# A Strassen level in layer 1 of four token groups, PSUM banks seeded by copies, and an engine order from a search

## The chip, the cores and the metric

The kernel runs on one core of one Trainium2 chip. The metric is the device time of one execution in microseconds (us), and less is better. Every kernel below was timed beside the kernel before on the same chip and in the same session. Where a ratio is given, it is the mean time of one kernel's fast runs over the mean time of the other's fast runs of the same rounds, so it is not quite the ratio of the medians that stand beside it. A run counts as slow when it is over 1.5% above the fastest of its kernel; slow runs are left out of ratios.

The five engines are TensorE (PE, with PEld its weight loads), VectorE (DVE), ScalarE (ACT), POOL and SyncE (SP). In the traces of this case each took its work in the order in which the program emitted it: the changed kernel and e12, which differ in the place of two small copies on POOL, have the same sequence of all 2807 matmuls and all 451 DVE instructions, although their times differ. So an instruction that waits holds up those that stand behind it on its engine: in e14 the last ACT result before a DVE gate was there at 36.74 us, but the gate began at 39.21, behind a sum that had waited 2.52 us for its load.

## The reference, cut to what matters

```python
q_p, k_p = phi(q), phi(k)              # relu, then times cos and sin of the position
kv  = einsum('bhsf,bhsd->bhfd', k_p, v)
num = einsum('bhsf,bhfd->bhsd', q_p, kv)
den = einsum('bhsf,bhf->bhs', q_p, k_p.sum(2)) + 1e-6
x   = (num / den), heads joined        # 4608 tokens x 512
h   = x @ w_in                         # layer 1: 512 -> 2048
g   = h * cos(h)
out = g @ w_out                        # layer 2: 2048 -> 512
```

There are 8 batches of 8 heads, 576 positions and 64 features. The kernel cuts the 4608 tokens into nine groups of 512: 0 to 6, "r" (what is left of the batches) and 7. The matmuls run in 16 bits, the result is 32-bit.

## The kernel before: the parts that matter here

The program first builds a list of operations (`op`), each with the engines that may take it and a cost on each, then puts them in an order, then emits them. Before, a greedy scheduler makes the order:

```python
def run(self, cold=0.0):                        # Plan.run, cut
    while ready:
        cand = []
        for o in ready:
            t = max([o.at] + [d.end + d.lat for d in o.deps])
            ...                                 # buffers: wait for a free one
            for e, us in o.alts.items():
                cand.append((max(t, clock.get(e, 0.0)), e, us, o, t))
        t0, e0 = min((c[0], c[1]) for c in cand)
        ...                                     # earliest start, then priority
```

Layer 1 is plain in all groups: 64 matmuls of 512 columns per group. Layer 2 is a Strassen product with seven products instead of eight in all groups but the first. It needs sums of blocks of g, and all of them are DVE's:

```python
def sums(g, c, n):
    ...
    nc.vector.tensor_tensor(out=out, in0=in0, in1=in1, op=op)   # 128 x 1024, f16, both inputs in SBUF
st[(c, n)] = op({"V": 0.69}, (1, i, c, n), lambda e, c=c, n=n: sums(g, c, n), ...)
```

The seven products end in three PSUM banks. The shared product is evicted once by ACT and then added to other banks by DVE:

```python
e1 = op({"A": 0.6},  EV, lambda e: cp(e, part(g, "s1"), ps[(g, "X")]), deps=[p1], acq=[s1])
e6 = op({"V": 0.69}, EV, lambda e: add(part(g, "u2"), g, "Y", "s1"), deps=[p6, e1], ...)
...                                             # e7, e5, e4, e3: adds of DVE too
```

## Time and profile before

The time is 303.36 us (median of 3, 303.26 to 305.72).

| what | value | seen in |
|---|---|---|
| TensorE busy | 280.1 us of a span of 298.7 (94%) | the page |
| DVE, ACT, POOL busy | 233.7, 175.6, 102.0 us | the page |
| last matmul ends | 293.9 us | the trace |
| TensorE idle between matmuls after 14 us | 15.8 us, none of it after 200 us | sum over the trace |

The first lines of the page: busy time, share and number of instructions of each engine, then the busy share in tenths in 40 slices, and the clock granted to TensorE.

```profile
span 298.7 us, 6583 instructions
PE 280.1 (94%) x2565; PEld 201.3 (67%) x2565; DVE 233.7 (78%) x450; ACT 175.6 (59%) x303; POOL 102.0 (34%) x107
...
PE   8879999899969987999979999999999999999993
...
PEclk9979999999999999999999999999999999999998
```

TensorE is close to full, and its clock is whole from the fourth slice to the last but one. A change that takes matmul work away should shorten this kernel, as long as the other engines keep up.

The groups of instructions by line and form show what two kinds of DVE work cost: line, engine, operation, output and inputs, count, then busy time and mean ns.

```profile
L309 DVE TENSOR_TENSOR s<-g 128x1024 f16<-128x1024 f16 x14 | 10.4, 744 | 0.1
...
L309 DVE TENSOR_TENSOR g<-g,s 128x1024 f16<-128x1024 f16 x14 | 9.5, 704 | 0.3 <-PE PX L337 0.2
...
L181 DVE TENSOR_SCALAR kp<-km,CS 128x512 f16<-128x512 f32 x28 | 15.5, 590 | 0.3 <-DMA km<-in_k_dram 0.2
```

A sum of 1024 elements costs 0.68 to 0.74 us. TensorE's longest waits are small (what it waited for, us in total, times, longest):

```profile
PE N L228 <- DVE x L241: 2.8, 2, 2.1
PE M L279 <- ACT xT L159: 2.6, 1, 2.6
PE PY L337 <- DVE s L309: 2.2, 2, 1.6
```

### The profile page before, as it was taken

How to read it: one execution, taken by the hardware profiler on the slowest of the kernel's cores; microseconds unless marked ns; L12 is line 12 of the kernel's file. 1: busy time of each engine (PE TensorE's matmuls, PEld its weight loads, DVE VectorE, ACT ScalarE, POOL GpSimd, SP SyncE). 2: the span in 40 equal slices, each digit the busy share in tenths (PEclk: the TensorE clock that was granted, in tenths of full speed). 3: DMA queues.
4: the chain of work that ended last, by engine and by line, in shares of the span. 5: the costliest groups of instructions: out<-in, count | busy, mean ns of one | idle time of the engine just before them, and what ended most of it. 6: DMA issues, size and time to landing. Idle time of an engine off the chain costs nothing.

```text
span 298.7 us, 6583 instructions
## 1 busy us (share of the span) xinstructions
PE 280.1 (94%) x2565; PEld 201.3 (67%) x2565; DVE 233.7 (78%) x450; ACT 175.6 (59%) x303; POOL 102.0 (34%) x107
## 2 busy tenths in 40 slices
PE   8879999899969987999979999999999999999993
PEld 8768856688855555566646666776666666566782
DVE  1878888899995798887869798987786786768661
ACT  2846748599379797679489497634433443443210
POOL 1370004396191686287077194011002001100500
PEclk9979999999999999999999999999999999999998
DMA  7799995897899999999999999715202100200213
GB/s 218 264 163 203 204 362 183 279 308 120 273 274 235 356 232 169 283 278 203 322 256 202 238 369 195 141 47 151 35 0 94 48 1 32 111 2 0 91 52 140
DMA packets 77086, 53.29 MB, mean 178 GB/s; under 512 B 46080, under 2 KB 74752, under 8 KB 77056
## 3 DMA queue, kind: packets, MB, share of 16 engines
q1 hardware_dynamic: 69760, 39.73, 55.2%
q0 software_dynamic: 6848, 12.59, 16.6%
q10 hardware_dynamic: 448, 0.57, 0.5%
q8 instruction: 20, 0.33, 0.5%
q14 instruction: 10, 0.08, 0.1%
HBM read 36.74 MB, written 9.44 MB: 155 GB/s over the span
## 4 chain that ended last, share of the span: by engine, by line
PE 55%; DMA 16%; DVE 10%; POOL 5%; SPq 5%; ACT 4%; issue 3%; ACTq 0%; DVEq 0%
PE M L279 26%; DMA vm<-in_v_dram 13%; PE PY L337 8%; PE PZ L337 6%; PE PX L337 5%; PE M L376 5%; POOL qp L181 4%; DMA qm<-in_q_dram 3%; PE KV L219 2%; DVE g L292 2%; SPq L171 2%; DVE x L241 2%; PE TP L263 2%; DVE s L309 2%; SPq L269 1%
## 5 line engine op out<-in xcount | busy, mean ns | idle before, releaser
L279 PE MATMUL M<-xT,w_in_sb 128*128 128x512 f16 (+1 forms) x640 | 120.2, 336 | 2.9 <-ACT xT L159 2.6
L286 ACT ACTIVATE ch<-M 128x512 f32<-128x512 f32 x144 | 84.9, 595 | 60.8 <-PE M L279 58.7
L292 DVE TENSOR_TENSOR g<-M,ch 128x512 f16<-128x512 f32 x128 | 85.8, 687 | 27.0 <-ACT ch L286 26.1
L279 PEld LDWEIGHTS <-w_in_sb 128*128 128x128 f16 x704 | 67.3, 98 | 46.6 <-issue 3.1
L181 POOL TENSOR_SCALAR qp<-qm,CS 128x512 f16<-128x512 f32 x29 | 60.0, 2074 | 31.0 <-DMA qm<-in_q_dram 27.0
L337 PEld LDWEIGHTS <-g 128*128 128x128 f16 x560 | 54.1, 98 | 11.5
L369 POOL DMA_DIRECT2D out_dram<-ost x14 | 7.8, 558 | 98.6 <-DVE ost L351 42.5
L179 ACT ACTIVATE kp<-km,CS 128x512 f16<-128x512 f32 x52 | 35.1, 715 | 0.2
L179 ACT ACTIVATE qp<-qm,CS 128x512 f16<-128x512 f32 x40 | 26.9, 713 | 11.9 <-DMA qm<-in_q_dram 11.9
L337 PE MATMUL PX<-w_out_sb,g 128*128 128x256 f16 x224 | 27.6, 273 | 0.0
L241 DVE TENSOR_TENSOR x<-N,rec 128x512 f16<-128x512 f32 (+1 forms) x44 | 26.1, 594 | 1.7 <-DVE rec L237 0.2
L337 PE MATMUL PY<-WT,g 128*128 128x256 f16 x224 | 27.2, 273 | 0.0
L337 PEld LDWEIGHTS <-s 128*128 128x128 f16 x224 | 21.4, 98 | 7.1 <-DVE s L309 2.8
L161 POOL CAST V<-vm 128x512 f16<-128x512 f32 (+1 forms) x22 | 13.9, 664 | 15.9 <-DMA vm<-in_v_dram 15.9
L228 PE MATMUL N<-kvz,qT 128*128 128x65 f16 x256 | 14.7, 196 | 2.3 <-DVE x L241 2.1
L228 PEld LDWEIGHTS <-qT 128*128 128x128 f16 x256 | 12.6, 100 | 6.1 <-issue 3.5
L337 PE MATMUL PY<-WT,s 128*128 128x256 f16 x112 | 14.1, 273 | 2.2 <-DVE s L309 2.2
L181 DVE TENSOR_SCALAR kp<-km,CS 128x512 f16<-128x512 f32 x28 | 15.5, 590 | 0.3 <-DMA km<-in_k_dram 0.2
L292 DVE TENSOR_TENSOR gr<-M,ch 128x512 f16<-128x512 f32 x16 | 10.9, 689 | 5.7 <-ACT ch L286 5.5
L219 PE MATMUL KV<-V,kp 128*128 128x65 f16 x320 | 12.9, 196 | 2.5 <-DVE kp L181 0.7
L279 PE MATMUL M<-xR,w_in_sb 128*128 128x512 f16 x64 | 15.1, 379 | 0.0
L219 PEld LDWEIGHTS <-kp 128*128 128x128 f16 x320 | 11.7, 99 | 4.7 <-issue 2.4
(70 smaller groups left out, 287.7 us busy)
## 6 DMA issues: line engine op xcount, KB each, us to landing
out_dram<-ost POOLq DMA_DIRECT2D x28, 256.0 KB, 4.1
qm<-in_q_dram SPq DMA_DIRECT2D x8, 640.0 KB, 5.3
km<-in_k_dram SPq DMA_DIRECT2D x8, 640.0 KB, 7.0
qm<-in_q_dram SPq DMA_DIRECT2D x8, 512.0 KB, 5.8
km<-in_k_dram SPq DMA_DIRECT2D x8, 512.0 KB, 8.8
vm<-in_v_dram SPq DMA_DIRECT2D x6, 640.0 KB, 8.1
vm<-in_v_dram SPq DMA_DIRECT2D x6, 512.0 KB, 8.9
w_in_sb<-in_moe_w_in_dram POOLq DMA_DIRECT2D x4, 512.0 KB, 9.0
```

The costliest lines, as they stand in the source:

```text
L161: (nc.vector if eng == "V" else nc.gpsimd).tensor_copy(out=out, in_=in_)
L179: nc.scalar.activation(out=dst, in_=src, func=AF.Relu, scale=sc)
L181: (nc.vector if eng == "V" else nc.gpsimd).tensor_scalar(out=dst, in0=src, scalar1=0.0, scalar2=sc, op0=ALU.max, op1=ALU.mult)
L219: nc.tensor.matmul(tile_[:, n, hh, :], lhsT=kps[b][:, t, h].rearrange("p g d -> p (g d)"), rhs=V1[:, t, h, :], start=(t == 0), stop=(t == NT))
L228: nc.tensor.matmul(tile_[:, n, hh, :], lhsT=qT(p, t)[:, h, :], rhs=kvzs[p][:, h, :], start=(i == 0), stop=(i == len(parts) - 1))
L241: nc.vector.tensor_tensor(out=dst, in0=tile_[:, :, :, 0:D], in1=rec.unsqueeze(3).broadcast_to((P, nb, HB, D)), op=ALU.mult)
L279: nc.tensor.matmul(ps[key][:, n, :], lhsT=w_in_sb[:, c, j * P:(j + 1) * P], rhs=x[:, c, s0:s1], start=(c == 0 and n == 0), stop=(c == NCT ...
L286: nc.scalar.activation(out=ps[("ch", key)], in_=ps[key].rearrange("p j s -> p (j s)"), func=AF.Sin, bias=math.pi / 2.0, scale=1.0)
L292: nc.vector.tensor_tensor(out=dst, in0=m, in1=ps[("ch", key)].rearrange("p (j s) -> p j s", s=m.shape[2]), op=ALU.mult)
L337: nc.tensor.matmul(ps[(g, bank)][:, i, :], lhsT=lhs[:, j, i * P:(i + 1) * P], rhs=rhs[:, j], start=(first and i == 0 and j == 0), stop=(j ...
L369: e0.dma_start(out=five[:, t0:t0 + 2, :], in_=blocks(ost, n))
L376: nc.tensor.matmul(ps[("M2", t)], lhsT=gts[0][:, j, t * P:(t + 1) * P], rhs=w_out_sb[:, j, :], start=(j == 0), stop=(j == NJT - 1))
```

## The change

The intent has four parts. A Strassen level is put into layer 1 of the last four groups (seven products of half size for eight). The first group's layer 2 becomes Strassen too. Where a shared product was added afterwards by DVE, it is now copied into a PSUM bank by ACT or DVE, and the next matmuls add to it. And the order is no longer computed: it is a fixed text, `ORDER`, from a long annealed search. The core of the diff:

```diff
-    def run(self, cold=0.0):
-        ...                                    # the greedy scheduler
+    def run(self):
+        return [(self.ops[int(x.rstrip("VAG"))], x.lstrip("0123456789"))
+                for x in ORDER.split()]
+ORDER = """
+115 818 25 230 180 184 24 229 342 22 883 21 40V 42V 41A 44V 43A 60 46A 61V 62 63V 48A 35V 32A
+...                                            # 1481 places; V, A, G: DVE, ACT, POOL
+"""
...
+    def tt(eng, out, in0, in1, op):
+        (nc.vector if eng == "V" else nc.gpsimd).tensor_tensor(out=out, in0=in0, in1=in1, op=op)
...
-        nc.vector.tensor_tensor(out=out, in0=in0, in1=in1, op=op)      # sums
+        tt(eng, out, in0, in1, op)
...
+    STR = {5, 6, "r", 7}                       # groups with Strassen in layer 1
...
+    WSUM = {"V": 1.24, "G": 4.7}
+    XSUM = {"V": 0.42, "G": 1.3}
+    SUM0 = {"V": 0.72, "G": 2.45}              # costs of a sum on DVE and on POOL
+    CGATE = {"V": 0.7, "G": 1.3}
...
+            def y_seed(e, qd=qd):              # seeds a bank by a copy
+                bank_tile(g, qd, "Y")
+                cp(e, ps[(g, qd, "Y")], ps[(g, qd, "X")])
...
+            def z_add(e, qd=qd):
+                tt(e, ps[(g, qd, "Z")], ps[(g, qd, "Y")], ps[(g, qd, "p5")], ALU.add)
...
-    layer2_plain(lambda t, n: (1, 1, t, n))
+    layer2(0, lambda i: (1, 1, i))
```

In the order, 57 operations with two inputs, sums and gates, stand on POOL. In what follows, "order" means this text, with the choice of engine that it also makes.

## The prediction

> **What bounds the kernel now.** The page gives TensorE 94% of a 298.7 us span, VectorE (DVE) 78%, ScalarE (ACT) 59%, POOL 34%. In TensorE's timeline, steady runs take 0.216 us per matmul of 512 columns and 0.1086 per 256. By that count layer 1 is 576 x 0.216 = 124.3 us, layer 2 of the first group 64 x 0.216 = 13.8, Strassen layer 2 of eight groups 8 x 112 x 0.1086 = 97.3, attention and transposes about 27: 263 us. The stream begins at 15.8 us (loads) and ends at 294.0, so 15 of 278 us are lost. TensorE's waits name about 12 of them, all before 190 us: xT at 87-90 (2.6), sums at 110-114 (2.9), the numerator at 152 (2.1). From 190 to 281 us the windows show TensorE 100%, DVE 76%, ACT 40%. After the last matmul: 0.69 us eviction, about 4.0 us store.
>
> **What the change does.**
> 1. Layer 1 of four groups: 64 x 512 columns become 112 x 256: 13.8 -> 12.2 us, four times: -6.6 us.
> 2. Layer 2 of the first group by Strassen: -1.7 us.
> 3. Two covering matmuls: +0.4 us. [...] I expect a right result.
> 4. Per quad four more PSUM passes: 64 x 0.6 to 0.69, about +42 us on ACT and DVE. Layer 2 keeps seven evictions per group, five now plain copies that ACT can take. Counting the new order by the trace's durations: DVE 234 -> 256 us, ACT 176 -> 207.
> 5. About 42 sums (1024 elements) and 11 gates go to POOL; the trace has no such operation. [...] some DVE sums (0.70 us now) will stretch.
> 6. The searched order replaces the greedy one, with finer q buffers; I expect it to remove half of the 12 us of waits. The last eviction is split by rows: -0.4 us.
>
> **How much is critical.** TensorE is the limit nearly throughout, so 1 to 3 count fully (-7.9). The new passes lie where 24% of DVE and 60% of ACT are free, but each quad is a chain of matmul, copy, matmul, add, matmul; with DVE at 90% I expect new waits of 1 to 3 us after 190 us.
>
> **Sum.** Span: 15.8 start + 255 matmuls + 8 lost + 4.3 end = 283. The timed median stood 4.7 us above the profiled span (303.36 against 298.7); so 288 us, 5% less. Range 283.5 to 295. Chances: faster 0.94, within 2% 0.05, slower 0.01.
>
> **What would show it.** 1-2: 112 matmuls per group at 0.109 us. 4: DVE 245-265 us, ACT 200-215. 5: [...] some DVE sums above 0.75 us. 6: TensorE's waits between 16 and 190 us about 6 us; the stream starting near 16 us and ending near 278.
>
> **What would make it wrong.** POOL sums far slower than estimated, or locking DVE, so that layer 2 waits for sums (292 and more); the fixed order meeting late DMA (loads land 5 to 12 us after issue) with no freedom to do other work; or a search that removed nearly all waits (284).

The sum: 15.8 + 255 + 8 + 4.3 = 283 us of span, and 288 us of time. Neither the time of POOL's sums nor the stretching of DVE's had a term in it. That some DVE sums stretch was an expectation then; the trace after shows it (744 ns before, 1605 after).

## More of the kernel before

The profile is of a run of its own, which took 300.70 us.

No instruction of POOL has two inputs in SBUF in this kernel.

## The result, and the profile after

The result is right, and the kernel is slower: 333.21 us (median of 4, 330.40 to 335.41) against 303.31 in the same session. The ratio of the fast runs is 1.095, with a 95% interval of 1.082 to 1.108. The profile is of the slow run (335.41 us), so its span is 1 to 5 us too long for the three fast ones. The page after:

```profile
span 333.6 us, 7212 instructions
PE 289.2 (87%) x2807; PEld 229.9 (69%) x2807; DVE 269.7 (81%) x451; ACT 189.1 (57%) x349; POOL 210.0 (63%) x161
...
PE   8769953879999999999699949999999799789893
...
PEclk9979997698999999999899989999999799979998
```

TensorE is no longer full: there are holes near 50, 160 and 195 us and smaller ones near 260 and 285, and after each of them the granted clock falls too (to between 0.6 and 0.9 of full in a slice of the page, where the kernel before has 0.9 or more from the fourth slice to the last but one). The same groups as above, after the change, and the POOL sums that are new:

```profile
L340 DVE TENSOR_TENSOR g<-M,ch 128x512 f16<-128x512 f32 x102 | 67.4, 683 | 8.0 <-ACT ch L389 7.2
...
L340 POOL TENSOR_TENSOR s<-s,g 128x1024 f16<-128x1024 f16 x10 | 21.9, 2188 | 5.5 <-DVE s L340 5.1
...
L219 DVE TENSOR_SCALAR kp<-km,CS 128x512 f16<-128x512 f32 x32 | 21.4, 697 | 1.0 <-DMA km<-in_k_dram 1.0
...
L340 DVE TENSOR_TENSOR s<-g 128x1024 f16<-128x1024 f16 x9 | 14.4, 1605 | 0.2
...
L340 DVE TENSOR_TENSOR g<-g,s 128x1024 f16<-128x1024 f16 x8 | 10.0, 1248 | 0.1
...
L418 DVE TENSOR_TENSOR w_out_sb<-w_out_sb 128x1024 f16<-128x1024 f16 x2 | 5.1, 2608 | 0.0
```

The same DVE sum went from 0.74 to 1.6 us, a sum of w_out blocks takes 2.6 us, and the relu products (kp) went from 590 to 697 ns. The gates, which take one input from PSUM, kept their 683 ns (687 before). So DVE as such did not become slower. Sorting the DVE instructions of this trace by what POOL did at the same time shows the pattern (mean ns, or each value where there are few):

| DVE instruction | POOL not computing | POOL in a two-input sum | POOL in a tensor_scalar |
|---|---|---|---|
| sum s<-g, both inputs in SBUF | 691 | 1398, 3633, 5287 | 681 |
| tensor_scalar kp | 478 | 1387 (two instructions) | 707 |
| gate g<-M,ch, one input in PSUM | 686 | 682 | 681 |

The other traces say the same. Taken over all 16, DVE's sums of 1024 elements over g and s take 685 ns where POOL does nothing (307 sums, none over 694), 684 beside memsets alone (35), 795 beside a tensor_scalar alone (104; median 683, at most 1334) and 1698 beside two-input sums alone (48). So a tensor_scalar of POOL, though it reads SBUF, blocks a sum little (795 ns against 685); a POOL instruction with two inputs is what costs (1698).

The timeline shows how it happens (start, duration, engine, instruction; in brackets the idle time before it and what ended it):

```profile
40.91 2.12 POOL L340 TENSOR_TENSOR s<-s,g 128x1024 f16<-128x1024 f16 x1
...
42.14 3.63 DVE L340 TENSOR_TENSOR s<-g 128x1024 f16<-128x1024 f16 x1
...
43.12 2.11 POOL L340 TENSOR_TENSOR g<-g 128x1024 f16<-128x1024 f16 x1
...
45.83 1.05 PE L438 MATMUL PZ<-WT,s 128*128 128x256 f16 x8 [2.99 <-DVE s L340]
...
46.30 5.14 DVE L418 TENSOR_TENSOR w_out_sb<-w_out_sb 128x1024 f16<-128x1024 f16 x2
```

The DVE sum issued at 42.14 while POOL held a sum until 43.03. It did not run then either: POOL's next sum began at 43.12, and the DVE sum ended at 45.77, 0.5 us after that one. So it seems to have run only when both were over. TensorE stood for 3 us. Its longest waits after:

```profile
PE TP L311 <- DVE qp L219: 4.8, 1, 4.8
PE PX L438 <- DVE SD L199: 4.4, 1, 4.4
PE PX L438 <- DVE gr L340: 3.3, 1, 3.3
PE SD L438 <- DVE s L340: 3.3, 3, 2.1
PE PZ L438 <- DVE s L340: 3.0, 1, 3.0
```

All are waits for DVE. Two of them name neither a sum nor a gate, but a qp and a copy that seeds a bank (SD); these stood on DVE behind blocked sums, the qp behind the w_out sums of 46.30, the copy behind this one:

```profile
192.49 5.29 DVE L340 TENSOR_TENSOR s<-g 128x1024 f16<-128x1024 f16 x1
...
193.02 2.13 POOL L340 TENSOR_TENSOR s<-s,g 128x1024 f16<-128x1024 f16 x1
...
195.10 2.11 POOL L340 TENSOR_TENSOR g<-g 128x1024 f16<-128x1024 f16 x1
...
197.70 0.69 DVE L199 COPY SD<-PX 128x512 f32<-128x512 f32 x1
...
198.44 1.86 PE L438 MATMUL PX<-w_out_sb,g 128*128 128x256 f16 x8 [4.44 <-DVE SD L199]
```

This sum began 0.53 us before the first of the two POOL sums (192.49 against 193.02) and ended 0.57 us after the second. So back to back sums of POOL can hold up one DVE sum several times.

After some idle stretches TensorE ran at half clock in this trace: the record of the granted clock has 0.5 for 3.41 us from 20.32, 74.94, 163.68, 197.81, 262.67 and 293.39 us, and for 10.24 us from 54.45. Six of these seven began in or shortly after one idle stretch of TensorE: of 1.79 us (to 20.75), 4.78 (to 53.85), 2.35 (to 164.38), 4.44 (to 198.43), 2.07 (to 262.73) and 3.34 us (to 293.48). The one from 74.94 came after three short ones, 1.77 us together. No limit can be read from that: an idle stretch of 2.99 us in the same trace (to 45.83 us), and two of 2.60 and 2.12 us in the kernel before (to 89.91 and 153.91), brought none.

To add this up, I took TensorE's matmuls of each trace from 14 us on, start to start, and split that time into the columns at the steady rate of these traces (0.216 us per 512), idle stretches over 0.15 us, and what matmuls took longer because the granted clock was 0.5. "DVE blocked" is the time of DVE's instructions with all inputs in SBUF beyond their unblocked duration. All in us:

| kernel | median time | matmuls | idle | half clock | DVE blocked |
|---|---|---|---|---|---|
| before | 303.3 | 260.6 | 15.8 | 1.1 | 5.9 |
| after | 333.2 | 253.6 | 45.9 | 12.1 | 39.7 |

To name what is in the 39.7: about two thirds are sums, most of the rest relu products (kp, qp). The last matmul ends 34.8 us later in the profiled run: 7.0 us less matmul work, 30.1 more idle, 11.0 more at half clock, 0.7 of small change. The Strassen level took away what it should. The idle time gave it back four times over.

### The profile page after: what moved, and what is told of

It reads as the page before. It is cut to its first block, busy times and chain, and to the rows that moved or that the text cites. A ratio compares the mean times of both kernels' runs of the same rounds, so it can differ in the third digit from the quotient of the medians.

```text
span 333.6 us, 7212 instructions
## 1 busy us (share of the span) xinstructions
PE 289.2 (87%) x2807; PEld 229.9 (69%) x2807; DVE 269.7 (81%) x451; ACT 189.1 (57%) x349; POOL 210.0 (63%) x161
## 4 chain that ended last, share of the span: by engine, by line
PE 42%; DVE 23%; DMA 18%; issue 6%; ACT 5%; POOL 3%; SPq 1%; ACTq 0%; DVEq 0%; POOLq 0%
PE M L327 9%; PE SD L438 7%; DVE g L340 6%; DMA w_out_sb<-in_moe_w_out_dram 6%; PE M L383 5%; PE PZ L438 5%; DMA km<-in_k_dram 5%; PE PX L438 4%; PE SD L383 3%; DVE kp L219 3%; DMA out_dram<-ost 3%; DMA vm<-in_v_dram 3%; PE YZ L383 3%; ACT ch L389 2%; PE KV L255 2%
## 5 line engine op out<-in xcount | busy, mean ns | idle before, releaser
L389 ACT ACTIVATE ch<-M 128x512 f32<-128x512 f32 x108 | 63.0, 595 | 50.9 <-PE M L383 26.0
L327 PE MATMUL M<-xT,w_in_sb 128*128 128x256 f16 (+1 forms) x448 | 78.2, 324 | 3.3 <-DMA w_in_sb<-in_moe_w_in_dram 2.2
L340 DVE TENSOR_TENSOR g<-M,ch 128x512 f16<-128x512 f32 x102 | 67.4, 683 | 8.0 <-ACT ch L389 7.2
L217 ACT ACTIVATE qp<-qm,CS 128x512 f16<-128x512 f32 x44 | 29.9, 715 | 10.4 <-DMA qm<-in_q_dram 7.6
L219 POOL TENSOR_SCALAR qp<-qm,CS 128x512 f16<-128x512 f32 x14 | 28.9, 2072 | 9.4 <-DMA qm<-in_q_dram 7.0
L219 POOL TENSOR_SCALAR kp<-km,CS 128x512 f16<-128x512 f32 x12 | 25.0, 2092 | 3.4 <-DMA km<-in_k_dram 3.4
L340 POOL TENSOR_TENSOR s<-s,g 128x1024 f16<-128x1024 f16 x10 | 21.9, 2188 | 5.5 <-DVE s L340 5.1
L383 PEld LDWEIGHTS <-WS 128*128 128x128 f16 x192 | 18.9, 101 | 5.5 <-issue 1.5
L199 POOL CAST V<-vm 128x512 f16<-128x512 f32 (+1 forms) x22 | 15.3, 724 | 11.4 <-DMA vm<-in_v_dram 11.3
L340 POOL TENSOR_TENSOR g<-g 128x1024 f16<-128x1024 f16 x10 | 22.4, 2244 | 0.0
L438 PE MATMUL PZ<-WT,s 128*128 128x256 f16 x128 | 17.3, 281 | 5.3 <-DVE s L340 3.0
L219 DVE TENSOR_SCALAR qp<-qm,CS 128x512 f16<-128x512 f32 x22 | 16.9, 782 | 5.3 <-DMA qm<-in_q_dram 5.3
```

Of the source, the lines that this page charges most:

```text
L199: (nc.vector if eng == "V" else nc.gpsimd).tensor_copy(out=out, in_=in_)
L217: nc.scalar.activation(out=dst, in_=src, func=AF.Relu, scale=sc)
L219: (nc.vector if eng == "V" else nc.gpsimd).tensor_scalar(out=dst, in0=src, scalar1=0.0, scalar2=sc, op0=ALU.max, op1=ALU.mult)
L327: nc.tensor.matmul(ps[key][:, n, :], lhsT=w_in_sb[:, c, j * P:(j + 1) * P], rhs=x[:, c, s0:s1], start=(c == 0 and n == 0), stop=(c == NCT ...
L340: (nc.vector if eng == "V" else nc.gpsimd).tensor_tensor(out=out, in0=in0, in1=in1, op=op)
L383: nc.tensor.matmul(ps[(g, qd, bank)][:, i, :], lhsT=lhs[:, c, 2 * qd + i, :], rhs=rhs[:, c, :], start=(first and i == 0 and c == 0), stop= ...
```

## The experiments

Theory LOCK: POOL's sums block DVE's, and TensorE waits for DVE. Rivals: POOL itself is late with its sums; the fixed order and its chains of matmul, copy, add are worse than the greedy order even without the lock; the extra work of the level cannot be hidden at all; batch 1's loads come too late.

### e1: POOL without its sums

In the changed kernel each two-input operation of POOL becomes two tiny copies and two memsets of the output, about as long and in the same place. Its output is wrong, which doesn't matter for the time.

```diff
+        for x in (in0, in1):
+            nc.gpsimd.tensor_copy(out=out[..., 0::P], in_=x[..., 0::P])
+        for _ in range(2):
+            nc.gpsimd.memset(out, 0.01)
-        nc.gpsimd.tensor_tensor(out=out, in0=in0, in1=in1, op=op)
```

> The changed kernel with each of POOL's 57 two-input operations replaced by two tiny copies (which keep the waits for both inputs) and two memsets of the output: POOL stays busy about as long (2.1 to 2.3 us for 1024 elements), but hardly reads. Wrong result on purpose. Theory LOCK (a POOL operation that reads two SBUF tensors blocks VectorE operations with two SBUF inputs): VectorE sums back to 0.69 us, none above 1.3 us next to such a POOL operation, VectorE busy about 235 us in place of 270, TensorE gaps below 20 us in place of 36, time 292 to 305. Rival ORDER/CHAINS (the fixed order and the longer matmul-copy-matmul-add chains cost the time by themselves): time stays within 325 to 336 although the sums are short. Rival POOL-LATE (POOL is simply too slow to deliver its sums in time): time also stays above 320, since POOL is as busy as before.

Measured: 314.56 us (311.61 to 315.82), ratio 1.036 (1.029 to 1.044). POOL was no less busy (221.4 us against 210.0). DVE fell from 269.7 to 241.1 us, blocked time from 39.7 to 10.6:

```profile
L341 DVE TENSOR_TENSOR s<-g 128x1024 f16<-128x1024 f16 x9 | 6.2, 688 | 0.3
...
L346 POOL MEMSET s<- 128x1024 f16 x34 | 33.1, 973 | 2.0
```

So 18.6 us of the loss (333.2 to 314.6) go with POOL's reads, though POOL works as long as ever. But 11.6 us against the kernel before remain, where LOCK expected at most 2. TensorE's idle time is still 30.4 us, where LOCK expected less than 20. All three expectations missed: the lock is most of it, not all.

### e2: the same sums on DVE

The 57 operations get the letter V for G in the fixed order, nothing else is moved.

```diff
-155V 165 178A 171V 172 181G 166A 173 179V 199 174A 343 192V 236 200 167V 182G 175V 210 201A 238
+155V 165 178A 171V 172 181V 166A 173 179V 199 174A 343 192V 236 200 167V 182V 175V 210 201A 238
```

> The changed kernel, same order, but the 57 two-input operations of POOL run on VectorE at the same places. LOCK: VectorE's sums are 0.69 us each, but VectorE carries about 39 us more real work in place of some 34 us of blocking, so it becomes the limit itself: VectorE busy 270 to 285 us, time 320 to 335, i.e. no cure. POOL-LATE: POOL no longer delays anything, time falls below 310. ORDER/CHAINS: the same order on a fuller VectorE, time 335 or more.

Measured: right result, 318.04 us (315.35 to 320.42), ratio 1.046 (1.039 to 1.054). POOL falls to 97.9 us and DVE takes 57 instructions more, yet its busy time falls:

```profile
PE 282.3 (89%) x2807; PEld 224.7 (71%) x2807; DVE 266.5 (84%) x508; ACT 189.5 (60%) x349; POOL 97.9 (31%) x104
```

DVE does all the sums itself in 3 us less than it took for its own share beside POOL, and the kernel is 15 us faster. In this order POOL's help was worth less than nothing. All three expectations missed in the time: LOCK, by 2 us, with its 320 to 335; POOL-LATE with below 310; ORDER/CHAINS with 335 or more.

### e3 and e4: sums, or writes, added to the kernel before

The kernel before gets 64 useless POOL operations, one for every second gate from the 18th on: a sum of 1024 elements on a scratch tile (e3), or two memsets of it (e4), which read nothing.

```diff
+        count[0] += 1
+        if count[0] > 16 and count[0] % 2 == 0:
+            nc.gpsimd.tensor_tensor(out=junk, in0=junk, in1=junk, op=ALU.subtract)   # e3
+            nc.gpsimd.memset(junk, 0.25)                                             # e4, twice
```

> The kernel before, with 64 useless sums of 1024 fp16 elements on POOL, on a scratch tensor that nobody reads (one after every second gate in the order). LOCK: VectorE's sums that meet one rise from 0.68 to 1.3 us and more, while PSUM-reading gates stay at 0.69; VectorE busy up by 10 to 25 us, and the time is up by 4 to 20 us more than in the run with writes in their place. ORDER/CHAINS and POOL-LATE: the same time as the run with writes, within 2 us.

> The kernel before, with 64 pairs of memsets of 1024 fp16 elements on POOL (about 1.9 us a pair) in place of the useless sums: POOL as late, nothing read. LOCK: VectorE sums stay at 0.68 to 0.75 us, and the time is 303 to 312, what POOL's own lateness costs. POOL-LATE: as slow as the run with sums.

Measured: e3 345.08 us, ratio 1.139 (1.129 to 1.148); e4 329.45 us, ratio 1.087 (1.081 to 1.092); both results right. DVE's own sums in e3, with POOL's added ones:

```profile
L297 POOL TENSOR_TENSOR junk<-junk 128x1024 f16<-128x1024 f16 x64 | 130.0, 2032 | 2.5
...
L312 DVE TENSOR_TENSOR g<-g 128x1024 f16<-128x1024 f16 x14 | 20.9, 1495 | 0.0
```

and in e4:

```profile
L298 POOL MEMSET junk<- 128x1024 f16 x64 | 61.5, 961 | 3.7
...
L313 DVE TENSOR_TENSOR g<-g 128x1024 f16<-128x1024 f16 x14 | 9.7, 695 | 0.0
```

With POOL about equally busy (234.7 us in e3, 222.0 in e4), the reading sums block DVE by 50.9 us and the writes by 7.3 (5.9 in the kernel before). That is the lock, shown in a kernel without the change. It costs 15.6 us of time here, within the 4 to 20 that LOCK expected between the two; DVE's busy time rose by 43.0 us in e3, where 10 to 25 were expected. The other 26 us of e4 were not expected (303 to 312 us): POOL's own useful work (V, qp) comes late, and TensorE waits 8.5 us for V. A busier POOL has a price of its own where something waits for it.

### e5 and e6: the same work in an order that counts the lock

I wrote a small model of the engines with the lock and the half clock in it, and searched for an order of the changed kernel's operations. The three small marker copies on POOL that hold back batch 1's loads were put together as one operation; the work is otherwise the same, with 44 two-input operations still on POOL in e5.

```diff
+                            mark.append(op({"G": 0.55}, (0, 1), lambda e: markers(),
+                                           deps=[w_land[NG + 1]] + feats0))
-115 818 25 230 180 184 24 229 342 22 ...
+...                                            # another ORDER
```

> The changed kernel with the same arithmetic and 44 two-input operations still on POOL, but a new fixed order: searched by replaying the dependency graph with one more rule, that a VectorE operation with two SBUF inputs waits for a running two-input POOL operation, and with a half-speed TensorE after an idle gap. The three small copies that release the loads of the second batch stand together. LOCK: the loss was the collision, so an order that avoids it recovers it: VectorE excess of the sums below 12 us, TensorE gaps 15 to 28 us, time 290 to 302, below the kernel before. CHAINS (matmul-copy-matmul-add chains and a seventh product per quad cost the time by themselves): time stays at 310 or more, as in the run with writes in place of the POOL sums.

> A second order from the same search with another random start: as the first, 290 to 302 if the rule and not the luck of one order makes the difference.

Measured: e5 311.47 us (ratio 1.025, 1.019 to 1.031), e6 321.03 us (1.054, 1.047 to 1.060). Both are faster than the changed kernel by 12 to 22 us and both miss what LOCK expected; CHAINS's "310 or more" fits both. The blocked time of DVE fell to 11.0 and 23.0 us (e6's profile is of a slow run, so its figure is a hint only). I found a fault in my search: a transfer could take a place that its issuing instruction did not have.

### e7 and e8: transfers tied to their issue

> The changed kernel's work once more, every matrix product, sum, copy and transfer (only the three small marker copies on POOL that release the batch-1 loads stand together as one, as in e5), in a second order of my own. The search for e5 and e6 had let a transfer start at a place in the order that its issuing instruction did not have, so those two orders were worse on the chip than in the search (296 to 300 us when evaluated properly, measured 311 and 321). In this search each transfer is tied to its issue; and it counts the lock (a two-input sum of DVE in SBUF waits for a two-input sum of POOL) and the half clock after an idle stretch. 51 two-input sums stay on POOL. Theory ORDER-AND-LOCK (the extra time of the changed kernel comes from an order that was laid out as if DVE and POOL did not disturb each other, not from the Strassen level as such): 285 to 297 us, faster than before, DVE excess over its unblocked durations below 8 us, idle stretches of TensorE together below 22 us, low clock after the first 15 us below 15 us. Rival LOAD (the extra sums and copies of the level cost more DVE, ACT and POOL time and longer chains than any order can hide): not below 303 us.

> The same as e7 from another seed of the same search; 50 two-input sums on POOL. ORDER-AND-LOCK: 285 to 297 us, within 4 us of e7. LOAD: not below 303 us. If the two differ by more than 6 us, the order's luck on the chip is larger than what the search counts, and neither theory is settled by them alone.

Measured: 320.77 us (1.057) and 311.17 us (1.024): ORDER-AND-LOCK missed again, and LOAD's "not below 303 us" fits. The medians differ by 9.6 us, and by the expectation of e8 that settles neither theory; two of e7's four runs count as slow, and the other two took 315.03 and 319.47 us. In e8 DVE is hardly blocked (9.6 us) and the half clock costs 3.0, so what is left is idle time: 11.3 us of it before 50 us, against 3.7 in the kernel before. The trace shows batch 1's loads issued from 27.3 us on, among the weight loads (33.9 us in the kernel before), and TensorE waiting 3.2 us for w_in and 3.1 us for what stood behind it.

### e9, e10 and e11: weights first, judged under disturbance

The eight weight loads stand in a fixed sequence, the search lets batch 1's loads wait for the seventh, and it judges each order over several draws of disturbed durations and landing times. The `deps` of the diff steer the search alone: on the chip the marker copies still read a block of the sixth load, and in e10 batch 1's q was issued at 34.6 us, between the landings of the sixth (34.2) and the seventh (36.7).

```diff
-                                           deps=[w_land[NG + 1]] + feats0))
+                                           deps=[w_land[NG + 2]] + feats0))
...
-        wi_op = op({"G": 0.8}, ..., lambda e, n=n: weights(n), deps=[held])
+        wi_op = op({"G": 0.8}, ..., lambda e, n=n: weights(n), deps=[wi_op])   # n in 0 2 3 1 4 5 6 7
```

> The changed kernel's work once more, in a third order of my own. What e7 and e8 showed: their searched orders let batch 1's loads start at 27 us, among the weight loads, so weights landed late and TensorE waited 3.2 us for w_in and 3.1 us behind it (the kernel before starts them at 33.9 us), and tight places of the order lost 1 to 4 us each where a transfer or a POOL instruction came a little later than reckoned. In this search the eight weight loads stand in a fixed sequence ahead of batch 1's loads, and every order is judged over five draws of disturbed durations and landing times, the lock and the half clock counted as before. 46 two-input sums stay on POOL. By the same judgement the orders of e5, e6 and the changed kernel's own come out at 311, 320 and 351 us (measured 311, 321, 333), this one at 291. ORDER-AND-LOCK: 288 to 300 us, at or below the kernel before; TensorE idle stretches below 24 us, those of the first 50 us below 7 us. LOAD (the level's own extra work cannot be hidden): not below 303 us.

> As e9, another seed; 51 two-input sums on POOL. ORDER-AND-LOCK: 288 to 300 us, within 5 us of e9. LOAD: not below 303 us.

> The changed kernel's work in a fourth order of my own, searched from e10's with what e9 and e10 showed put in: the last two w_out loads landed 2 us later than reckoned (18.5 us after issue against 15), batch 1's v loads 4 us later (7.8 against 3.7), and each order is judged over seven draws of disturbed durations and landing times instead of five. 46 two-input sums stay on POOL. By that judgement e9's order and e10's come out at 298 and this one at 290; those two measured 308 and 302. ORDER-AND-LOCK: 292 to 300 us, faster than before by 1 to 4%. LOAD, in the weaker form that e10 leaves it (an order can bring the changed kernel's work to the time of the kernel before, but not lower): 300 to 306 us.

Measured: e9 308.42 us (1.013, 1.006 to 1.019), e10 301.87 us (0.991, 0.984 to 0.998), e11 312.81 us (307.38 to 318.62, no ratio given). So the very work of the changed kernel runs in 302 us in one order and in 333 in another. The theory that the level's work cannot be brought to the time of before is dead. But the search cannot tell which of its orders will do it: e11 was judged the best of the three and is slower than e10. Four of its six runs count as slow; its two fast runs (307.38 and 308.06 us) are level with e9's and 6 us above e10's. Its six runs spread over 11 us, those of the kernel before in that session over 5.7. ORDER-AND-LOCK missed for e9 and e11, and for e10 by 2 us at its upper end of 300. LOAD's "not below 303 us" fits e9 and fell with e10; its weaker form (300 to 306 us) missed for e11 as well.

### e12: only the marker copies moved

The changed kernel in its own order, with the three marker copies together where the first one stood.

> The changed kernel in its own order, one thing moved: the three small marker copies on POOL that release batch 1's q, k and v loads stand together where the first one stood, so the k and v loads no longer wait behind POOL's sums (in the changed kernel q is issued at 35.8 us, k at 41.0, v at 43.2; in the kernel before all three between 33.9 and 40.8). LATE-LOADS (a good part of the 12 us that e1 left comes from these loads): 322 to 328 us against the 330 to 334 of the changed kernel's own fast runs, k and v issued before 40 us. LOCK-ONLY (the loads are not what TensorE waits for; DVE behind POOL's sums is): no change beyond 2 us, 329 to 335 us.

Measured: 333.62 us (332.23 to 335.51), the same as the changed kernel's 333.21. The move did what it should to the loads: k was issued at 36.5 us instead of 41.0 and v at 38.4 instead of 43.2. TensorE waited elsewhere instead, 6.7 us at 47.3 us for a kp of ACT. That is what LOCK-ONLY expected. But the loads landed hardly earlier: the two of k at 44.9 and 46.4 us instead of 45.8 and 47.3, those of v about 1.2 us earlier. So e12 shows that the late issue of these loads is not where the time of the changed kernel went; a trial in which they land much earlier is missing.

### e13 and e14: the longest wait of e10 taken out, and e10 again

In e10 a weight sum that needs the last w_out load stands on DVE in front of a gate that frees a PSUM bank. In e13 two such sums stand five gates later.

```diff
-... 154A 159V 190V 189V 192V 155V ...  247 249 193V 272G ...  277G 171V 262A 264A 194V ...
+... 154A 159V 190V 189V 155V ...       247 249 272G ...       277G 171V 192V 193V 262A 264A 194V ...
```

> e10's kernel with two of its 1481 places changed: the first two weight sums over the second half of w_out, on DVE, stand five gates later, behind the gate of block 5. In e10 the first of them waited 2.4 us for its load, and the gates behind it, one of which frees the bank for the next matmul, waited with it: TensorE idle for 3.5 us at 37.3 us. ORDER-MEETS-LATE-TRANSFER: that stretch falls below 1.5 us and e13 is 1.5 to 3.5 us below e14 (e10 again on the same chip), 298 to 300.5 us. LOAD: the stretch only moves (to a wait for the same weight sums, or for batch 1's features), and e13 is within 1 us of e14.

> e10's kernel, unchanged, on the chip of e13 and with more rounds. ORDER-AND-LOCK: 300 to 304 us, ratio to before 0.98 to 1.0, as in e10. If its luck with transfers was particular to that one session, as e11's scatter (307 to 319) suggests it might be: above 305 us.

Measured: e14 301.52 us, ratio 0.990 (0.985 to 0.995); e13 301.30 us, ratio 0.988 (0.982 to 0.994). The timeline of e14 where the wait is:

```profile
38.60 0.69 DVE L408 TENSOR_TENSOR WT<-w_out_sb 128x1024 f16<-128x1024 f16 x1 [2.52 <-DMA w_out_sb<-in_moe_w_out_dram]
...
39.21 0.68 DVE L330 TENSOR_TENSOR g<-M,ch 128x512 f16<-128x512 f32 x1
...
39.94 2.29 PE L317 MATMUL M<-xT,w_in_sb 128*128 128x256 f16 x10 [3.84 <-DVE g L330]
```

and of e13:

```profile
39.86 0.68 DVE L330 TENSOR_TENSOR g<-M,ch 128x512 f16<-128x512 f32 x1
...
40.46 0.68 DVE L408 TENSOR_TENSOR WT<-w_out_sb 128x1024 f16<-128x1024 f16 x1
...
42.06 2.56 ACT L207 ACTIVATE qp<-qm,CS 128x512 f16<-128x512 f32 x4 [2.67 <-DMA qm<-in_q_dram]
```

The sums no longer hold up the gate, and the wait of 3.8 us is gone. TensorE now runs dry 5 us later (at 41.4 us instead of 36.1) and waits 2.7 us for qp, which waits for batch 1's q. The wait moved, and e13 is within 1 us of e14, as the rival said. (Its profile fell in a slow run, so only this stretch is read from it.) e10 itself is confirmed: about 1% below the kernel before.

The page of e14, the best profiled run of the changed kernel's work:

```profile
span 297.9 us, 7175 instructions
PE 273.7 (92%) x2807; PEld 223.5 (75%) x2807; DVE 236.0 (79%) x440; ACT 198.3 (67%) x357; POOL 183.2 (62%) x164
...
PEclk9999979999999999999999999999999999999998
```

POOL still has 183 us of work here, and DVE takes 34 us less than in the changed kernel. The runs of the changed kernel's work in the same split as above (us), each from its profiled run; e6 and e13, whose profiles are of slow runs, and e11 and e12 are left out, and the profile of "after" is of a slow run too:

| kernel | median time | matmuls | idle | half clock | DVE blocked |
|---|---|---|---|---|---|
| before | 303.3 | 260.6 | 15.8 | 1.1 | 5.9 |
| after | 333.2 | 253.6 | 45.9 | 12.1 | 39.7 |
| e1 (no reads by POOL's sums) | 314.6 | 253.6 | 30.4 | 7.1 | 10.6 |
| e2 (sums on DVE) | 318.0 | 253.6 | 35.8 | 5.2 | 7.0 |
| e5 | 311.5 | 253.6 | 29.6 | 4.0 | 11.0 |
| e7 | 320.8 | 253.5 | 32.5 | 6.9 | 20.8 |
| e8 | 311.2 | 253.6 | 29.0 | 3.0 | 9.6 |
| e9 | 308.4 | 253.5 | 28.5 | 5.0 | 11.8 |
| e10 | 301.9 | 253.2 | 24.2 | 2.5 | 14.9 |
| e14 (e10 again) | 301.5 | 253.2 | 22.8 | 1.5 | 14.2 |

e14 has 7.4 us less matmul work than before and 7.0 us more idle time. Of that, 5.7 us lie before 50 us (9.4 against 3.7) and 5.6 after 200 us (5.6 against 0); between them it has less than before.

## Why the prediction was wrong

The prediction said 288.0 us (283.5 to 295), faster with 0.94. Measured: 333.21 us, slower. The term of its sum that failed is "8 lost": TensorE lost 45.9 us in idle stretches and 12.1 at half clock. Two steps stand behind it, 5 (the blocked sums, which were not priced) and 6 (the waits that the order was to remove).

- **What bounds the kernel before**: right. TensorE 94%, about 15 us lost; the trace gives 15.8.
- **Steps 1 to 3, the matmul work, -7.9 us**: right. The ideal time of the matmuls fell by 7.0 us in the profiled run, and in every order tried. The seeded banks gave right results in all runs that kept the arithmetic. Why they do was not tested by itself.
- **Step 4, the passes**: counted too high. DVE 256 us predicted, 269.7 measured, of which 39.7 are blocked time, so 230 unblocked, 2 more than in the kernel before (233.7 less 5.9); ACT 207 predicted, 189.1 measured. So the work of the passes itself is not what made the kernel slower.
- **Step 5, POOL's sums**: they took 2.18 to 2.28 us (the means of the four largest groups; POOL 210.0 us in all). The stretching came as expected: DVE's sums with both inputs in SBUF stretched (s<-g from 744 to 1605 ns), PSUM-reading gates did not (687 and 683 ns), and memsets of POOL, which only write, hardly block (e4, 695 ns for a DVE sum). What failed is the term for it in the sum. "Some DVE sums (0.70 us now) will stretch" was written down and priced at nothing. DVE's blocked time rose from 5.9 to 39.7 us; 29.1 us of it go when POOL's reads go (e1), and with them 18.6 us of the kernel's time.
- **Step 6, the order**: wrong. "I expect it to remove half of the 12 us of waits." Idle time went from 15.8 to 45.9 us, and without POOL's reads (e1) it is still 30.4. The cost table in the diff gives a DVE sum 0.72 us and a POOL sum 2.45 us, independent of each other. The search that made the order, if it used this table, filled both engines on that footing. On the chip the DVE sum that took 3.6 us at 42.14 was paid by TensorE with 3 us.
- **The half clock**: not in the prediction at all. It makes idle time dearer: 12.1 us in the changed kernel, beside its 45.9.
- **"How much is critical"**: the sentence "I expect new waits of 1 to 3 us after 190 us" was far too small: 18.4 us of idle time and 4.7 at half clock fall after 190 us, where the kernel before had none.
- **From span to time**: the 4.7 us were the difference between a median and the span of another run. The profiled run took 300.70 us for a span of 298.7, so 2.0 would have been right; this changes nothing in the outcome.

Of the risks named at the end, the first (POOL locking DVE) was the right one. Late transfers cost TensorE 3.2 us in e8 and 3.8 in e14; for the changed kernel no run shows what they cost. But the figure put on the first, "292 and more", and the chance of 0.01 for slower were not drawn from anything. With a lock whose cost was unknown, and no trace of it in the profile of before, that certainty had no ground.

What is shown and what is not: the lock is shown (e1, e3 against e4), as most of the loss: 18.6 of 29.9 us by e1, 15.2 by e2, which takes the sums from POOL in another way. That the rest, and even the whole, is a matter of order and not of the level is shown by e10 and e14, where the same work takes 302 us, with 51 of the 57 two-input operations still on POOL. Which property of the order makes it so is not settled. Nor was the work of the change run under the greedy scheduler, or the work of the kernel before in a searched order, so the level, the seeded banks and the search were never timed apart. The searched orders differ by 19 us among themselves for reasons that my model did not foresee, and the one wait that I took out (e13) moved. It also stays open whether the level can bring more than the 1% of e10: about 7 us of new idle time eat its 7 us, at the start and in the last 100 us. A version that beats both kernels exists (e10, and e13 in the same margin), by 1%, inside the 2% that counts as the same.

## What to carry to other kernels

Before giving POOL the sums that DVE has no time for, count which DVE instructions will meet them with all inputs in SBUF (here a DVE sum took 1698 ns beside POOL's two-input sums and 685 beside an idle POOL), and price the stretch in the sum, as blocked time and not as a remark. A cost table that lists engines as independent cannot see what one costs the other (39.7 us of DVE's time in the changed kernel), and here the error landed on the engine that bounds the kernel. When a change bundles new work with a new order, run the same work in another order before judging the work.
